# Batch 0's attention with fewer TensorE instructions and its local AV chunk by chunk; batch 1's v by two kinds of transfer

## The chip, the cores and the metric

The kernel runs on one core of a Trainium2 chip. The metric is the device time of one execution in microseconds; before the change the median of five runs is 331.19 us (329.89 to 333.34). Five engines take part: TensorE (PE; its weight loads are shown as PEld), VectorE (DVE), ScalarE (ACT), GpSimd (POOL) and SyncE (SP). Each works through its own list of instructions in order and waits for the others by semaphores. Transfers are issued by SyncE or by GpSimd and run on 16 DMA engines.

## The reference

Eight batches, eight heads, 576 tokens, head width 64. The attention is the sum of two softmax attentions: one over tokens averaged in groups of four (144 x 144), whose result is repeated four times, and one over the band of tokens less than four apart. Its output, 4608 tokens of 512, goes through two products with a gate between them.

```python
q_d = q.reshape(B, H, Sd, factor, D).mean(axis=3)        # likewise k_d, v_d; factor 4
out_up = np.repeat(sm_attn(q_d, k_d, v_d), factor, axis=2)
mask = np.abs(pos[:, None] - pos[None, :]) < factor
scores = np.where(mask, scale * q @ k.T, -1e9)
out_local = softmax(scores) @ v
x = (out_up + out_local)                                  # to (4608, 512)
h = x @ w_in                                              # (4608, 2048)
g = h * (1.0 / (1.0 + np.exp(-1.702 * h)))
out = g @ w_out                                           # (4608, 512)
```

## The kernel before

All matrix work is in bf16. The order of every engine's instructions is the order in which the program issues them (a manual schedule): nothing is moved by a scheduler.

**Tiling.** Of a batch, heads are taken in two groups of four ("qd", 0 and 1) for scores and in four pairs ("hp", 0 to 3) for the products with v. The local attention cuts the 576 tokens into ten blocks of about 57 queries with 64 keys: five chunks i, each with a half par 0 and a half par 1 that lie in the lower and upper 64 partitions. `scores` (L340) makes 80 small matmuls for a group, `scores_d` (L362) 24 for the averaged attention. `av_local` (L403) makes 20 matmuls for a pair, four per chunk, and `av_down` (L417) 20 for the averaged part. Both write one tile of PSUM; a column of ones in v gives the softmax's sum, and `normalise` (L439) divides on VectorE. The tiles of PSUM are PA[0..2], two banks each, and PM[0..1].

**Batch 0.** It has nothing to hide behind and is written out by hand (L712 to L800). k and q come by casting transfers from GpSimd, v by ten transfers from SyncE (`load_v`, L207: five chunks, two halves each). VectorE transposes k and q (`prep_1`, L256); GpSimd adds tokens in fours (`pool_qk`, L270). Constants come from iotas on GpSimd and comparisons on VectorE: the mask of the band, an identity `ident` of 64 columns, once in each half of the partitions, the selection matrix `psel` (`make_psel`, L164, and `end_psel`, L180) and the matrix `up` (`make_up` and `spread_up`). In batch 0 the band is made by TensorE: `bar_others` (L327) writes −1e6 outside the band into the tiles of scores by eight matmuls with `ident`, four for each half, and the scores add to it. v's chunks are cast to bf16 by ScalarE (0 and 1) and VectorE (2 to 4); `prep_vd_pe` (L306) makes the averaged v from all five chunks by 14 matmuls with `psel`, and ScalarE copies it to SBUF. Then come `av_local` and `av_down` of pairs 0 and 1, `scores_d` of the second group, pairs 2 and 3, and between them `turned` (L782): it transposes a pair's result, adds the repeated part by `transp_sum` (L477) and has it copied to `xT`, the input of the dense products. `warm(n)` (L570) issues n matmuls of 512 columns on zeros whose result is not used; it is called with 19, 5, 6 and 1.

**Dense products.** Group g of 512 tokens goes through `mm1` (w_in, L618; Silu on ScalarE, L629) and `mm2` (w_out, L674; copies on ScalarE, L659). The attention of batch g+1 is put between these matmuls at positions listed in POS (in POS_0 for g = 0, where `prep_vd_pe` of batch 1 stands at 52).

**Loads around group 0** (L808 to L823). GpSimd's list: w_in, k and q of batch 1, the first half of w_out, a memset of v4 (L740), then for g = 0 the adding in fours for batch 1, a one-element copy that waits for batch 1's v to land in part (the gate, L814, chunk 3), the second half of w_out, five casts of v 1's chunks, and the loads of k and q of batch 2. SyncE's list: v of batch 0, v of batch 1 (ten transfers behind a gate on the first part of w_out), then v of batch 2, which waits until the casts have read v 1.

Of the kernel before, what the change touches and what calls it, by code (L numbers as in the profile page):

```python
# [19 lines left out]
def kernel(  # L20
# [32 lines left out]
        tc.tile_pool(name="psum", bufs=1, space=bass.MemoryType.PSUM)  # L53
    )

    ident = consts.tile([128, 64], BF16, name="ident")
    mask = consts.tile([128, 2, 300], BF16, name="mask")
    w_in_bf = persist.tile([128, n_dmc, d_ff], BF16, name="w_in_bf")
    w_out_bf = persist.tile([128, n_ffc, d_model], BF16, name="w_out_bf")
# [28 lines left out]
    PSEL = [(4, 2), (2, 1), (0, 0), (1, 0), (1, 1), (3, 1), (3, 2)]  # L88

    dm = consts.tile([128, 60], FP32, name="dm")  # L90
    di = consts.tile([128, 64], FP32, name="di")
    dr = consts.tile([128, 1], FP32, name="dr")
    du = consts.tile([128, UP], FP32, name="du")
    ub = consts.tile([128, UP], BF16, name="ub")
# [13 lines left out]
    def iota_mask():  # L108
        for par in range(2):
            nc.gpsimd.iota(dm[halves[par]], pattern=[[-1, 60]], base=-4 * par,  # L110
                           channel_multiplier=1, **it)
        for par in range(2):
            nc.gpsimd.iota(di[halves[par]], pattern=[[-1, 64]], base=0,
                           channel_multiplier=1, **it)

    def iota_up():
        for par in range(2):
# [17 lines left out]
    def make_mask():  # L135
# [7 lines left out]
            in_=dm[:, None, :].to_broadcast([128, 10, 60]),  # L143
        )

    def make_ident(di):
        nc.vector.tensor_single_scalar(out=ident, in_=di, scalar=0.0, op=ALU.is_equal)

    def make_up():
        nc.vector.reduce_sum(out=rm, in_=ident[:, 0:48], axis=mybir.AxisListType.X)  # L150
        nc.vector.scalar_tensor_tensor(
            out=du, in0=du, scalar=-192.0, in1=du, op0=ALU.add, op1=ALU.mult
        )
        nc.vector.tensor_scalar(
            out=ub, in0=du, scalar1=0.0, scalar2=rm, op0=ALU.is_equal, op1=ALU.mult
        )
# [47 lines left out]
        load_1("k", k, kf, b, qd)  # L204
        load_1("q", q, qf, b, qd)

    def load_v(b, gate=None):  # L207
        t = ldp.tile([128, 5, H, D], FP32, name="vf", tag="vf")
        vf[b] = t
        if gate is not None:  # L210
            gate(t[0:1, 0, 0, 0:1])
        for i in range(5):
            for par in range(2):
                nc.sync.dma_start(
                    out=t[64 * par : 64 * par + 64, i],
                    in_=bass.AP(
                        tensor=v.tensor,
                        offset=v[b, 0].offset + (114 * i + KSTART[par]) * D,
                        ap=[[D, 64], [S * D, H], [1, D]],
                    ),  # L220
                )

    def load_v4(b):
        for kc in range(3):
# [100 lines left out]


    def bar_others(sp):  # L327
        for par in range(2):
            rows = slice(64 * par, 64 * par + 64)
            for r in range(4):  # L330
                nc.tensor.matmul(
                    sp[r // 2][rows, r % 2, 0:300],
                    lhsT=ident[rows, :],
                    rhs=off[rows, None, :].to_broadcast([64, 5, 60]),
                    start=True, stop=True,
                    tile_position=(64 * par, 64 * par),
                    skip_group_check=True,
                )

    def scores(b, qd, barred=False):  # L340
        sp = [ps_tile(), ps_tile()]
# [58 lines left out]
        av_down(b, hp, o)  # L400
        return o

    def av_local(b, hp, o):  # L403
        E, vb = es[hp], vbs[b % 2]
        for i in range(5):
            for par in range(2):
                for j in range(2):
                    pos = j if par == 0 else 1 - j
                    nc.tensor.matmul(  # L409
                        o[64 * pos : 64 * pos + 64, par, 65 * i : 65 * i + 65],  # L410
                        lhsT=E[64 * par : 64 * par + 64, j, 60 * i : 60 * i + 64],
                        rhs=vb[64 * par : 64 * par + 64, i, 2 * hp + j, :],
                        start=True, stop=True,
                        tile_position=(64 * par, 64 * pos),
                    )
# [34 lines left out]
    def transp(y, n=None):  # L450
        x = ps_tile(n)
        for i in range(5):
            for par in range(2):
                for j in range(2):
                    pos = j if par == 0 else 1 - j
                    c0 = 0 if (par == 1 or i == 0) else 3
                    c1 = 60 if (par == 0 or i == 4) else 57
                    nc.tensor.matmul(  # L458
                        x[64 * j : 64 * j + 64, par, 57 * i + c0 : 57 * i + c1],
                        lhsT=y[64 * pos : 64 * pos + 60, par, i, :],  # L460
                        rhs=ident[64 * pos : 64 * pos + 60, c0:c1],
                        start=True, stop=True,
                        tile_position=(64 * pos, 64 * j),
                    )
        for c2, xx in ((0, 0), (0, 1), (1, 0)):
            for j in range(2):
                pos = j if xx == 0 else 1 - j
                nc.tensor.matmul(
                    x[64 * j : 64 * j + 64, xx, 288 + 48 * c2 : 336 + 48 * c2],
                    lhsT=y[64 * pos : 64 * pos + 48, j, 5 + c2, :],  # L470
                    rhs=ident[64 * pos : 64 * pos + 48, 0:48],
                    start=True, stop=True,
                    tile_position=(64 * pos, 64 * j),
                )
        return x

    def transp_sum(y, x):  # L477
# [24 lines left out]
        for i in range(5):  # L502
            for par in range(2):
                for j in range(2):
# [3 lines left out]
                    nc.tensor.matmul(  # L508
                        x[par][64 * j : 64 * j + 64, 57 * i + c0 : 57 * i + c1],
                        lhsT=y[64 * pos : 64 * pos + 60, par, i, :],  # L510
                        rhs=ident[64 * pos : 64 * pos + 60, c0:c1],
                        start=False, stop=True,
                        tile_position=(64 * pos, 64 * j),
                        skip_group_check=True,
# [52 lines left out]

    def warm(n):  # L570
        if n:
            t = pm_tile()
            for _ in range(n):
                nc.tensor.matmul(  # L574
                    t, lhsT=wz[:, 0:128], rhs=wz, start=True, stop=True
                )

    def attention(b, slots=None):
# [139 lines left out]
    iota_up()  # L718
    fill()
    load_v(0, gate=after(kdT[1][0:1, SD, 0:1], nc.vector))  # L720
    warm(19)
    make_mask()
    make_ident(di)
    prep_1("k", 0, 0)
    prep_1("q", 0, 0)
    pool_qk(0, 0)
    sp = scores(0, 0, barred=True)
    exp_local(0, sp)
    prep_qk(0, 1)
    pool_qk(0, 1, "k")  # L730
    nc.gpsimd.tensor_copy(out=w_in_bf[0:1, 0, 0:1], in_=vf[0][0:1, 2, 0, 0:1])
    load_w_in(0, 512)
# [4 lines left out]
        load_qk(1, qd)  # L737
    load_w_out(0)
    load_w_out(1)
    nc.gpsimd.memset(v4[32:64], 0.0)  # L740
    make_psel()
    end_psel()
    make_up()
    warm(5)
    sd = scores_d(0, 0)
    prep_v(0, nc.scalar, i=slice(0, 1))
    exp_down(0, sd)
    sp = scores(0, 1, barred=True)
    exp_local(1, sp)
    prep_v(0, nc.scalar, i=slice(1, 2))  # L750
    spread_up()
    for i in range(2, 5):
        prep_v(0, nc.vector, i=slice(i, i + 1))
    warm(6)
    prep_vd_pe(0, PA[2])
    for hp in range(2):
        o[hp] = PA[hp]
        av_local(0, hp, o[hp])
    for hp in range(2):
        av_down(0, hp, o[hp])  # L760
        y[hp] = normalise(o[hp])
# [4 lines left out]
            func=AF.Exp, scale=inv_sqrt_d / 16.0,  # L766
        )
    nc.scalar.preload_act_table_set("silu_and_others")
    warm(1)
    o[2] = av(0, 2, 2)  # L770
    y[2] = normalise(o[2])

# [33 lines left out]
    for g in range(n_groups):  # L806
        b = g + 1
        if g == 0:  # L808
            prep_qk(1, 0)
            pool_qk(1, 0)  # L810
            prep_qk(1, 1)
            load_v(1, gate=after(w_out_bf[0:1, 0, 0:1], nc.vector))
            pool_qk(1, 1)
            nc.gpsimd.tensor_copy(  # L814
                out=w_out_bf[0:1, 8, 0:1], in_=vf[1][0:1, 3, 0, 0:1]
            )
            load_w_out(2)
            load_w_out(3)
            for i in range(5):
                prep_v(1, nc.gpsimd, i=slice(i, i + 1))  # L820
            for qd in range(NQ):
                load_qk(2, qd)
# [54 lines left out]
```

The softmax here doesn't subtract the row's maximum and nothing guards it: scores larger than these inputs give would overflow.

## Time and profile before

| | |
|---|---|
| median of five runs | 331.19 us |
| the profiled execution | 330.17 us |
| its span, first to last instruction | 328.4 us |
| TensorE busy | 96% of the span |
| granted TensorE clock, mean | 0.995 |
| ScalarE, VectorE, GpSimd busy | 56%, 40%, 42% |
| DMA, mean | 126 GB/s, 41.36 MB |

The profile shows one execution. A line such as `14.62 0.18 PE L351 MATMUL ... x1 [1.41 <-issue]` of the timeline reads: from 14.62 us on, 0.18 us long, TensorE executed line 351, once, after having been idle for 1.41 us; the arrow names what ended the idle time, and "issue" means that the engine waited for nothing which the profile shows. In a table of windows each row gives a stretch of time, its length, then the busy microseconds of each engine with the number of instructions, then the granted TensorE clock as a share of full speed, the busy share of the DMA engines and the GB/s. The chain in order of time gives start, length and what was at work in the chain that ended last.

The first 67 us hold the part in which TensorE has gaps: batch 0's attention until about 30.5 us, from where dense products run, and batch 1's attention between 42.7 and 67.3 us.

### The profile page before, as it was taken

To read this page: it belongs to the slowest core of one execution; us is meant where nothing else is said; L and a number is where in the kernel's file an instruction comes from. 1 tells how busy PE (TensorE), PEld (TensorE's weight loads), DVE (VectorE), ACT (ScalarE), POOL (GpSimd) and SP (SyncE) were. 2 spreads that over 40 slices of the span, in tenths; PEclk is the share of its full clock that TensorE was granted. 3 is DMA by queue.
4 is the path that set the end of the run, shared out by engine and by line. 5 is a ranking of instruction groups with operands and counts; after the bars stand their busy time and mean duration, and the time that the engine had idled before them with its cause. 6 is when DMAs were issued, how large, how long until landed. Compare 5 with 4: busy or idle time off the path is not lost.

```text
span 328.4 us, 11276 instructions
## 1 busy us (share of the span) xinstructions
PE 313.7 (96%) x5043; PEld 157.8 (48%) x5043; DVE 131.7 (40%) x215; ACT 184.1 (56%) x322; POOL 138.3 (42%) x168
## 2 busy tenths in 40 slices
PE   8777999899999999999999999999999999999995
PEld 3453455435554455445544554454444544444444
DVE  4872423670477037803680378125730560000000
ACT  2552882465926593658366836774576656415611
POOL 7890843069505960397039802990098000000000
PEclk9989999999999999999999999999999999999999
DMA  7999979999616980499139913992180100021011
GB/s 125 184 200 208 166 153 190 187 263 221 157 36 169 215 166 36 132 208 188 56 116 205 198 67 103 204 195 83 53 159 2 68 34 32 2 77 51 2 63 65
DMA packets 63552, 41.36 MB, mean 126 GB/s; under 512 B 44048, under 2 KB 54416, under 8 KB 63504
## 3 DMA queue, kind: packets, MB, share of 16 engines
q1 hardware_dynamic: 55056, 26.95, 34.5%
q0 software_dynamic: 8304, 13.63, 23.6%
q8 instruction: 39, 0.64, 0.8%
q14 instruction: 9, 0.07, 0.1%
q10 hardware_dynamic: 144, 0.07, 0.1%
HBM read 44.83 MB, written 9.44 MB: 165 GB/s over the span
## 4 chain that ended last, share of the span: by engine, by line
PE 91%; issue 3%; DMA 2%; DVE 2%; ACT 1%; POOL 1%; POOLq 0%; ACTq 0%; DVEq 0%
PE pm L618 36%; PE pm L674 36%; PE pa L351 4%; DMA qb<-in_q_dram 2%; PE pa L618 2%; PE pa L431 2%; PE pa L409 2%; PE pa L458 2%; PE pa L370 2%; PE pa L674 2%; PE pm L689 1%; PE pm L574 1%; PE pa L312 1%; ACT vd L321 0%; DVE xT L555 0%
## 5 line engine op out<-in xcount | busy, mean ns | idle before, releaser
L618 PE MATMUL pm<-xT,w_in_bf 128*128 128x512 bf16 x544 | 121.3, 379 | 0.7 <-DVE xT L561 0.7
L674 PE MATMUL pm<-w_out_bf,gT 128*128 128x512 bf16 x528 | 121.7, 380 | 0.0
L629 ACT ACTIVATE gT<-pm 128x512 bf16<-128x512 f32 x136 | 81.0, 598 | 45.3 <-PE pm L618 45.3
L618 PEld LDWEIGHTS <-w_in_bf 128*128 128x128 bf16 x576 | 55.6, 98 | 67.7 <-issue 1.4
L674 PEld LDWEIGHTS <-gT 128*128 128x128 bf16 x560 | 51.7, 98 | 59.5 <-issue 0.2
L276 POOL TENSOR_TENSOR pq<-kT 128x576 f32<-128x576 bf16 x16 | 18.5, 1157 | 103.6 <-DVE kT L260 95.4
L395 DVE TENSOR_TENSOR es<-es,mask 128x600 bf16<-128x600 bf16 x28 | 21.5, 785 | 92.3 <-ACT es L381 91.6
L659 ACT ACTIVATE osb<-pm 128x512 f32<-128x512 f32 (+2 forms) x35 | 20.7, 593 | 40.1 <-PE pm L674 36.1
L534 ACT COPY od<-pa 128x384 f32<-128x384 f32 (+1 forms) x56 | 18.4, 412 | 32.0 <-DVE y L444 18.7
L444 DVE TENSOR_TENSOR y<-pa,rc 128x896 bf16<-128x896 f32 x32 | 34.9, 1092 | 1.1
L555 DVE TENSOR_TENSOR xT<-pa,od 128x570 bf16<-128x570 f32 x28 | 21.1, 754 | 11.6 <-ACT od L534 11.5
L381 ACT ACTIVATE es<-pa 128x600 bf16<-128x600 f32 x32 | 19.8, 668 | 7.4 <-PE pa L351 7.2
L297 POOL TENSOR_TENSOR v<-v 112x512 f32<-112x512 f32 x18 | 22.8, 1266 | 0.0
L661 DVE TENSOR_SCALAR osb<-pm 128x128 f32<-128x128 f32 x1 | 0.3, 291 | 55.3 <-ACT osb L659 55.3
L260 DVE STREAM_TRANSPOSE kT<-kb 128x576 f32<-128x576 f32 x16 | 20.0, 1249 | 1.7 <-DMA kb<-in_k_dram 1.7
L260 DVE STREAM_TRANSPOSE qT<-qb 128x576 f32<-128x576 f32 x16 | 19.8, 1240 | 1.1 <-DMA qb<-in_q_dram 1.1
L276 POOL TENSOR_TENSOR pq<-qT 128x576 f32<-128x576 bf16 x16 | 18.4, 1148 | 0.0
L291 POOL CAST vb<-vf 128x2560 bf16<-128x2560 f32 (+1 forms) x11 | 17.2, 1592 | 0.0
L351 PE MATMUL pa<-qT,kT 32*64 32x60 bf16 x1280 | 14.4, 203 | 2.3 <-issue 1.4
L351 PEld LDWEIGHTS <-kT 32*64 32x64 bf16 x1280 | 12.3, 104 | 7.6 <-issue 6.3
L442 DVE RECIPROCAL rc<-pa 128x14 f32<-128x14 f32 x32 | 7.7, 240 | 20.5 <-PE pa L431 20.5
L300 POOL TENSOR_TENSOR vd<-v 112x256 bf16<-112x256 f32 x18 | 13.7, 759 | 1.4
(90 smaller groups left out, 246.5 us busy)
## 6 DMA issues: line engine op xcount, KB each, us to landing
vf<-in_v_dram SPq DMA_DIRECT2D x80, 128.0 KB, 5.3
out_dram<-osb SPq DMA_DIRECT2D x35, 256.0 KB, 2.0
v<-in_v_dram SPq DMA_DIRECT2D x36, 192.0 KB, 5.1
kb<-in_k_dram POOLq DMA_DIRECT2D x16, 288.0 KB, 6.3
qb<-in_q_dram POOLq DMA_DIRECT2D x16, 288.0 KB, 7.9
w_out_bf<-in_moe_w_out_dram POOLq DMA_DIRECT2D x4, 512.0 KB, 12.5
w_in_bf<-in_moe_w_in_dram POOLq DMA_DIRECT2D x2, 512.0 KB, 6.5
w_in_bf<-in_moe_w_in_dram POOLq DMA_DIRECT2D x1, 1024.0 KB, 10.6
```

Source lines behind the costliest of these rows:

```text
L260: nc.vector.transpose(out=t32.rearrange("p (i c) -> p c i", c=18), in_=store[b, qd].bitcast(FP32).rearrange("p (c d) -> p c d", c=18),)
L276: nc.gpsimd.tensor_tensor(out=t1, in0=sv[:, :, 0:2, :], in1=sv[:, :, 2:4, :], op=ALU.add)
L297: eng.tensor_tensor(out=t1[0:112], in0=x[:, :, 0:2, :], in1=x[:, :, 2:4, :], op=ALU.add)
L351: nc.tensor.matmul(sp[r // 2][64 * par : 64 * par + 64, r % 2, 60 * i : 60 * i + 60], lhsT=kT[b, qd][rows, k0 : k0 + 64, a], rhs=qT[b, qd] ...
L381: nc.scalar.activation(out=es[2 * qd + u][:, :, 0:300], in_=sp[u][:, :, 0:300], func=AF.Exp, scale=inv_sqrt_d,)
L395: nc.vector.tensor_tensor(out=ev, in0=ev, in1=mask, op=ALU.mult)
L444: nc.vector.tensor_tensor(out=y, in0=ov[:, :, :, 0:D], in1=rc.to_broadcast([128, 2, 7, D]), op=ALU.mult,)
L555: eng.tensor_tensor(out=sub(xT[hp], t0 + 3, (57, 2), (114, 5), (1, 57)), in0=sub(x, 3, (509, 2), (57, 5), (1, 57)), in1=sub(od, 3, (57, 2) ...
L618: nc.tensor.matmul(acc, lhsT=w_in_bf[:, dmc, ffc * 128 : (ffc + 1) * 128], rhs=xT[dmc][:, g * TG : g * TG + TG], start=(dmc == 0), stop=(d ...
L629: nc.scalar.activation(out=gT[:, ffc, :], in_=acc, func=AF.Silu, scale=GELU_SCALE)
L659: eng.activation(out=osb, in_=ap, func=AF.Copy, scale=1.0 / GELU_SCALE)
L674: nc.tensor.matmul(ops[t], lhsT=gT[:, ffc, t * 128 : (t + 1) * 128], rhs=w_out_bf[:, ffc, :], start=(ffc == 0), stop=(ffc == n_ffc - 1),)
```

## The change

The identity becomes one of 128 columns over all 128 partitions (`id128`), and `ident(pos, n, c0, c1)` gives the 64-wide parts that the transposes read. `bar_others` then makes four matmuls over all partitions in place of eight over halves. `warm` is called with 11, 4 and 3 in place of 19, 5 and 6, the call with 1 is gone, and the first of the 11 reads `id128` as its weights; it stands behind `make_ident`. VectorE runs `make_psel` between the transposes of k and q of the second group. The cast of v 0's chunk 1 moves from ScalarE to VectorE. `av_local` of pairs 0 and 1 is issued for chunks 0 to 3 ahead of `prep_vd_pe`, and for chunk 4 after it. Of v 1, SyncE loads chunks 0 to 2 and GpSimd casts them; chunks 3 and 4 come by four casting transfers that GpSimd issues (`load_vb`), straight into the bf16 tile. The gate of w_out's second half reads chunk 1 of v 1 in place of chunk 3. The memset of v4 moves in the source into the g = 0 branch; on GpSimd it stays between w_out's first half and the adding in fours.

```diff
-    ident = consts.tile([128, 64], BF16, name="ident")
+    id128 = consts.tile([128, 128], BF16, name="id128")
...
+    def ident(pos, n, c0, c1):
+        return id128[64 * pos : 64 * pos + n, 64 * pos + c0 : 64 * pos + c1]
...
+    def load_vb(b, i):
+        for par in range(2):
+            nc.gpsimd.dma_start(
+                out=vbs[b % 2][64 * par : 64 * par + 64, i, :, 0:D],
+                in_=bass.AP(
+                    tensor=v.tensor,
+                    offset=v[b, 0].offset + (114 * i + KSTART[par]) * D,
+                    ap=[[D, 64], [S * D, H], [1, D]],
+                ),
+            )
...
-        for par in range(2):
-            rows = slice(64 * par, 64 * par + 64)
-            for r in range(4):
-                nc.tensor.matmul(
-                    sp[r // 2][rows, r % 2, 0:300],
-                    lhsT=ident[rows, :],
-                    rhs=off[rows, None, :].to_broadcast([64, 5, 60]),
-                    start=True, stop=True,
-                    tile_position=(64 * par, 64 * par),
-                    skip_group_check=True,
-                )
+        for r in range(4):
+            nc.tensor.matmul(
+                sp[r // 2][:, r % 2, 0:300],
+                lhsT=id128,
+                rhs=off[:, None, :].to_broadcast([128, 5, 60]),
+                start=True, stop=True,
+                skip_group_check=True,
+            )
...
-    def av_local(b, hp, o):
+    def av_local(b, hp, o, chunks=range(5)):
...
-    def warm(n):
+    def warm(n, first=False):
         if n:
             t = pm_tile()
-            for _ in range(n):
+            for m in range(n):
                 nc.tensor.matmul(
-                    t, lhsT=wz[:, 0:128], rhs=wz, start=True, stop=True
+                    t, lhsT=id128 if first and m == 0 else wz[:, 0:128], rhs=wz,
+                    start=True, stop=True,
                 )
...
-    warm(19)
     make_mask()
     make_ident(di)
+    warm(11, first=True)
...
-    prep_qk(0, 1)
+    prep_1("k", 0, 1)
+    make_psel()
+    prep_1("q", 0, 1)
...
-    nc.gpsimd.memset(v4[32:64], 0.0)
-    make_psel()
     end_psel()
     make_up()
-    warm(5)
+    warm(4)
...
-    prep_v(0, nc.scalar, i=slice(1, 2))
     spread_up()
-    for i in range(2, 5):
+    for i in range(1, 5):
         prep_v(0, nc.vector, i=slice(i, i + 1))
-    warm(6)
+    warm(3)
+    for hp in range(2):
+        o[hp] = PA[hp]
+        av_local(0, hp, o[hp], range(4))
     prep_vd_pe(0, PA[2])
     for hp in range(2):
-        o[hp] = PA[hp]
-        av_local(0, hp, o[hp])
+        av_local(0, hp, o[hp], range(4, 5))
...
-    warm(1)
...
         if g == 0:
+            nc.gpsimd.memset(v4[32:64], 0.0)
+            load_vb(1, 3)
+            load_vb(1, 4)
             prep_qk(1, 0)
...
-            load_v(1, gate=after(w_out_bf[0:1, 0, 0:1], nc.vector))
+            load_v(1, gate=after(w_out_bf[0:1, 0, 0:1], nc.vector), chunks=range(3))
...
-                out=w_out_bf[0:1, 8, 0:1], in_=vf[1][0:1, 3, 0, 0:1]
+                out=w_out_bf[0:1, 8, 0:1], in_=vf[1][0:1, 1, 0, 0:1]
...
-            for i in range(5):
+            for i in range(3):
                 prep_v(1, nc.gpsimd, i=slice(i, i + 1))
```

## Prediction

> **What bounds the kernel now.** I read the page's first three parts, then the chain that ended last, then TensorE's timeline up to 67 us, then tables of windows. The page first: TensorE is busy 96% of the span, and it executes 10,088 instructions (5,043 weight loads, 5,043 matmuls, two others), which come in through a queue of their own.
>
> ```profile
> PE 313.7 (96%) x5043; PEld 157.8 (48%) x5043; DVE 131.7 (40%) x215; ACT 184.1 (56%) x322; POOL 138.3 (42%) x168
> q8 instruction: 39, 0.64, 0.8%
> ```
>
> 0.64 MB over 10,088 instructions is 63 bytes each, and over 39 packets 16 KB, so a packet is a page of 256 instructions. From 67 us on TensorE hardly pauses, and the change leaves that part's work as it is. What can be won lies before. The chain in order of time names two gaps there in which TensorE waits for nothing that the profile shows, and a third at 63 us:
>
> ```profile
> 13.21 1.41 issue
> 24.02 2.72 issue
> 63.31 0.89 issue
> ```
>
> TensorE's timeline shows what stops: the middle of a series without any dependence between its members.
>
> ```profile
> 14.62 0.18 PE L351 MATMUL pa<-qT,kT 32*64 32x60 bf16 x1 [1.41 <-issue]
> 23.77 0.25 PE L508 MATMUL pa<-ident,y 60*64 60x60 bf16 x6
> 26.74 0.31 PE L508 MATMUL pa<-ident,y 60*64 60x57 bf16 x14 [2.72 <-issue]
> ```
>
> Counted in the program, those two places are instructions 448 and 960, and the third is 2240: 448 + 2·256 and 448 + 7·256. They are page ends. The packets of the instruction queue fit: in the trace they start at 11.80, 18.51, 24.51 and 30.45 us, take 0.94 to 1.33 us, and TensorE resumes 1.5 and 1.3 us after the first and the third end. The three pages follow one another at about 6 us. [...] All this is while the DMA engines are full (share 1.0 to 1.2).
>
> [...]
>
> **Front part, step by step.** The change removes 42 instructions ahead of the dense products: 8+1+3+1 warming matmuls (26 instructions), 4 matmuls in each of two bar_others (16). Page ends stay at 448 and 960 of the count, and so fall on work that stood 42 later.
>
> *Stall of 1.41 us.* Instruction 448 is now in hp 0's fourth v chunk, work that has to wait for v's casts anyway. The stall in the scores goes. What is late next: DVE's order. make_psel (12.18 to 13.76, 1.58 us) moves ahead of the q 1 transpose, which could start at 11.07: k 1's is over at 10.05, so q 1's starts at 11.63, 0.56 us late, and scores(0, 1) end at 13.8 in place of 14.8. The casts of v on DVE no longer wait for the 1.97 us of L151, which sat beside POOL's 14.07 to 16.05; but v's last transfer lands at 16.91, so the last cast ends at 17.4 against 18.2. prep_vd_pe, ACT's copy (0.80) and av_down come 0.8 us earlier. ACT loses one cast of 0.61, DVE gains one of 0.42: both inside this wait. The wider iota, identity and reduce cost 0.1 each at most, beside loads.
>
> *Stall of 2.72 us.* It stood at 960; there now stands the work that ran at 27.73 (within turned(2), L484 from 27.52), so at the same arrival of the page 27.73 − 26.74 = 1.0 us is won. Against it: the first request. warm(11) now reads id128, ready at 4.5 us (L147 starts at 4.19, 0.29 us), where before TensorE started at 1.20. Behind that wait stand the bars and scores(0, 0), and behind those exp on ACT. Its clock rose at 4.85, 3.65 us after the start. From 4.6 at 0.43 us a matmul (half clock, as the nine before 4.85 show) to about 8.3, then 0.22, eleven end at 8.8; four full-width bars of 300 columns, 0.13 each, end at 9.3; scores(0, 0) begin 0.85 us after the 8.49 of before, the request goes out at 9.9, 1.0 us later. With three pages of 6 us behind it, 960 is there at 27.7, and the 1.0 us is spent. The range is wide: the clock can rise between about 6.5 and 9.7, which puts the sum between −0.7 and +0.8. I take 0. The earlier vd then only lengthens the waits at 704 (to 21.7) and 960 (24.2 to 27.7, 3.4 us).
>
> **The clock.** The windows before the dense part:
>
> ```profile
> core 0: us, PE busy (x) PEld busy (x) DVE busy (x) ACT busy (x) POOL busy (x), PEclk, DMA share, GB/s
> 11.68:15.09 3.41, 1.74 (x90) 1.17 (x86) 3.31 (x10) 2.22 (x4) 2.18 (x5) 1.00 0.97 165
> 15.09:18.50 3.41, 3.41 (x20) 1.60 (x17) 3.08 (x5) 1.94 (x3) 3.33 (x5) 0.50 1.02 158
> 25.33:28.74 3.41, 2.00 (x50) 1.21 (x50) 0.00 (x0) 1.13 (x6) 0.00 (x0) 1.00 1.12 209
> 28.74:32.16 3.42, 3.42 (x45) 1.77 (x44) 1.04 (x3) 0.99 (x6) 0.00 (x0) 1.00 1.11 210
> ```
>
> 1.74 us busy of 3.41 is followed by half clock, 2.00 by full. [...] In this execution the stall fell 1.31/1.41 across a border and the clock held; shifted, it loses a window at half clock, up to 1.7 us in dense work. That would explain why the profiled execution (330.17 = span 328.4 + 1.8 around it) lies 1.0 under the median of 331.19. After the change the stall of some 3.4 us brings the loss in nearly every execution, about 1.3 us. So from the profiled time +1.3, from the median +0.3. The fewer warming matmuls after 15 us cost at half clock only in stretches that wait for a page: nothing on the path.
>
> **Middle, 36 to 67 us.** For v 1, SyncE issues 6 transfers in place of 10 and POOL casts 3 chunks in place of 5 (0.62 each, −1.2 us on POOL). POOL issues four more (between 0.55 of kb and 0.84 of w_in each: 2.2 to 3.4 us), which wait in order for older transfers, the last landing at 31.09; POOL stands idle until 32.96 (8.12 us for DVE's kT), so this is covered; uncovered it would push pool_qk(1, 0) by up to 3.4 us, of which scores at 42.7 leave most free. The casting transfers queue behind w_out's, landed at 39.39; half a MB at about 200 GB/s makes 43, needed at 53.2. If casting in small pieces goes at half that rate, 45. The gate of w_out's second half opens on v 1's chunk 1 (42 to 43) instead of 3 (45.17), and the loads for batch 2 follow about 3 us earlier; no TensorE row waits for them, gain 0. The 2.65 us memset stays at its place in POOL's order.
>
> The page ends move by 42 here too. 1984 falls in the second tr instead of the first. Its request slips out of the dense products (50.1) into prep_vd_pe (53.5): 21 pairs at 0.216 us. With 6 us it is there at 59.7, wanted at 58.4: a stall of 1.3 us that did not exist, and 2240 asks after it, 0 to 0.8 us of stall in place of 0.89. Net +0.4 to +1.2; with less DMA traffic −0.9. I take +0.6.
>
> **Late.** Two gaps of the same kind, at 123.53 (0.37) and 224.46 (0.78), lie in av, at 4288 and 7872. 42 on, the page ends meet dense products 1 us later: −1.15; between −1.15 and 0 if other ends grow. I take −1.15.
>
> Sum from the median: 331.19 + 0 + 0.3 + 0.6 − 1.15 = 330.9; from the profiled time: 330.17 + 0 + 1.3 + 0.6 − 1.15 = 330.9.
>
> **Rivals.**
> *Faster, requests not late.* If the clock rises at 6.5 to 7, scores(0, 0) keep their 8.49, the page comes at 26.8 and 1.0 us is won; if the earlier transfers also shorten the pages near 60 us, another 0.8. 330.9 − 1.8 = 329.1. For it: the page latency at quiet DMA, in the later batches, is about 1.1 us to the packet against 3 to 4 here. Against: the engines stay full until 35 us.
> *Slower, the page of 1984.* One mechanism: its request moves 3.4 us later, because a dense stretch that covered it ends before it. It decides from a latency of 4.9 us (58.4 − 53.5); the page of 2240 took 6.9 in the same stretch. At 6.9 it costs 2.0, hands the full lateness to 2240, and nothing shrinks: +2.1 against the +0.6 taken, with the clock then falling once more (+0.8): 333.2.
> *It doesn't do what it says.* Half the removed instructions are warming ones beside waits; if the pages weren't the cause, nothing moves: 331.2, inside the first case.
>
> **Numbers.** About as before (330.9): 0.55; faster rival 0.22; slower rival 0.20 (333.2); v 1's casting transfers or something unseen late by 4 us or more (335): 0.03. 80% lies between 328.8 and 333.4. A measurement of this kernel can tell about 1% from no change, 3.3 us: faster by more (under 327.9) 0.08, the far end of the faster rival; slower by more (over 334.5) 0.07, the end of the slower one and the last case; within 0.85.
>
> **What would show it.** Right: no gap in scores(0, 1); scores(0, 0) at 9.0 to 9.8; a gap of over 3 us in turned(2), ending between 27 and 28.3, then a window at half clock; a gap in the second tr at 58 to 60; none at 123 and 224. Wrong: a gap at 960 under 2 us, or warm(11) ending by 7.5. What would upset the number: another page latency in the first 30 us, since three of them stand in a row.

## The result and the profile after

The change makes no difference that can be told: 331.3 us (median; 329.3 to 335.5) against 331.4 us for the kernel before, measured beside it, a ratio of 1.0004 with a 95% interval of 0.9991 to 1.0018. The ratios here and below leave out executions that took over 1.5% longer than the fastest of their kernel; the medians do not. The profiled execution took 330.80 us, span 329.0, against 330.17 and 328.4. The forecast was 330.9. That this is not the same as "nothing happened" shows already in the page. First TensorE's and the instruction queue's lines, then the granted clock in 40 slices of 8.2 us:

```profile
PE 313.5 (95%) x5022; PEld 158.5 (48%) x5022; DVE 132.2 (40%) x216; ACT 183.6 (56%) x321; POOL 140.7 (43%) x169
PEclk9857999999999999999999999999999999999999
q8 instruction: 39, 0.64, 0.9%
```

42 instructions are gone, and the clock is at 0.8, 0.5 and 0.7 in slices 2 to 4, where the kernel before had one short dip; its mean over the span is 0.979 in place of 0.995. The stalls have moved as well. The chain of after in order of time, those of its "issue" steps in which TensorE stood still (start, length):

```profile
28.48 0.59 issue
...
59.83 0.59 issue
...
90.58 0.22 issue
...
191.48 1.00 issue
```

Both long stalls of the front, 1.41 and 2.72 us, and those at 63, 123 and 224 us are gone. One of 0.59 is left at instruction 960, one of 0.59 is new in the second `tr`, one of 1.00 is new at 191, and a short one of 0.22 at 91. TensorE's timeline of after says what stands in the place of the first two; the bracket gives idle time and releaser:

```profile
4.44 0.61 PE L586 MATMUL pm<-wz,id 128*128 128x512 bf16 x1 [4.44 <-DVE id L148]
...
9.12 0.84 PE L363 MATMUL pa<-qT,kT 32*64 32x60 bf16 x80
...
13.67 0.83 PE L363 MATMUL pa<-qT,kT 32*64 32x60 bf16 x80 [1.63 <-DVE qT L275]
16.82 0.27 PE L421 MATMUL pa<-vb,es 64*64 64x65 bf16 x4 [0.96 <-DVE vb L306]
17.62 0.83 PE L421 MATMUL pa<-vb,es 64*64 64x65 bf16 x24 [0.53 <-DVE vb L306]
20.98 0.87 PE L443 MATMUL pa<-vd,ed 48*64 48x65 bf16 x40 [0.64 <-ACT vd L336]
29.07 0.16 PE L506 MATMUL pa<-up,y 128*64 128x3 bf16 x1 [0.59 <-issue]
```

These are waits for VectorE, for v's casts and for ScalarE's copy of vd. Together with a clock that stays at half speed they bring TensorE late to instruction 960, so that the page, there at about 29 us, is hardly waited for. The table of windows (columns as before: length, busy time of the engines, clock, DMA) shows how long half clock holds:

```profile
11.30:14.72 3.42, 1.79 (x95) 1.30 (x87) 3.38 (x8) 1.41 (x3) 2.24 (x4) 1.00 1.35 179
14.72:18.13 3.41, 1.84 (x28) 0.66 (x30) 3.41 (x5) 2.23 (x3) 3.31 (x4) 0.50 1.01 147
18.13:21.54 3.41, 2.77 (x79) 2.06 (x76) 0.31 (x1) 0.80 (x1) 3.41 (x7) 0.50 1.13 167
21.54:24.96 3.42, 3.22 (x111) 2.57 (x107) 3.23 (x6) 2.19 (x3) 3.38 (x3) 0.50 1.16 211
24.96:28.37 3.41, 3.41 (x95) 2.19 (x86) 1.93 (x3) 1.70 (x9) 0.99 (x2) 0.50 1.12 211
28.37:31.78 3.41, 2.82 (x70) 1.67 (x64) 0.00 (x0) 0.83 (x4) 1.36 (x2) 1.00 1.12 211
```

Four windows at half clock, 14.71 to 28.37 us, against one, 15.09 to 18.50, before. In both kernels half clock follows a window busy for about half its length (1.74 before, 1.79 after). Before, the next window was busy throughout (3.41 of 3.41: warming matmuls and `prep_vd_pe`) and full clock came back at once. After, the next three are busy 54%, 81% and 94%, none of them brings it back, and the fourth, busy 100%, does.

Where the two profiled executions stand against one another (start of the same matmul in both, us):

| | before | after | later by |
|---|---|---|---|
| scores(0, 0) | 8.49 | 9.12 | 0.63 |
| last matmul of scores(0, 1) | 14.62 | 14.29 | −0.33 |
| last small matmul ahead of the dense products | 30.38 | 31.72 | 1.34 |
| first scores of batch 1 | 42.69 | 44.03 | 1.34 |
| prep_vd_pe of batch 1 | 53.21 | 54.42 | 1.21 |
| last matmul | 324.6 | 325.5 | 0.9 |

So the front loses 1.34 us in this pair, the middle and the late part win 0.4, and 0.3 more is won behind the last matmul.

### The profile page after: what moved, and what is told of

It is laid out like the page before. It is cut to its first block, busy times and chain, and to the rows that moved or that the text cites. A ratio compares the mean times of both kernels' runs of the same rounds, so it can differ in the third digit from the quotient of the medians.

```text
span 329.0 us, 11227 instructions
## 1 busy us (share of the span) xinstructions
PE 313.5 (95%) x5022; PEld 158.5 (48%) x5022; DVE 132.2 (40%) x216; ACT 183.6 (56%) x321; POOL 140.7 (43%) x169
## 4 chain that ended last, share of the span: by engine, by line
PE 90%; DMA 2%; SPq 2%; issue 2%; DVE 2%; ACT 1%; DVEq 0%; ACTq 0%
PE pm L631 36%; PE pm L687 35%; PE pa L363 3%; PE pa L421 2%; PE pa L631 2%; PE pa L443 2%; DMA vf<-in_v_dram 2%; SPq L218 2%; PE pa L470 2%; PE pa L382 2%; PE pa L687 2%; PE pm L702 1%; PE pa L327 1%; PE pa L496 1%; PE pa L480 0%
## 5 line engine op out<-in xcount | busy, mean ns | idle before, releaser
L407 DVE TENSOR_TENSOR es<-es,mask 128x600 bf16<-128x600 bf16 x28 | 20.6, 751 | 91.4 <-ACT es L393 90.6
L306 POOL CAST vb<-vf 128x2560 bf16<-128x2560 f32 (+1 forms) x9 | 16.1, 1806 | 0.0
L421 PE MATMUL pa<-vb,es 64*64 64x65 bf16 x640 | 12.8, 202 | 2.8 <-DVE vb L306 1.5
```

Of the source, the lines that this page charges most:

```text
L407: nc.vector.tensor_tensor(out=ev, in0=ev, in1=mask, op=ALU.mult)
```

## The experiments

The theory at the outset was that of the prediction: pages of instructions set the stalls, the clock follows them, and v 1's transfers weigh nothing. The rivals: that the clock, through the waits for VectorE and the casts, sets the front; and that one of the edits loses by its place what another wins. All kernels do the whole computation. The mean clock of an execution tells how long it ran at half: one window of 3.41 us takes 0.0052 off it (the profiled executions: 0.995 with one such window before, 0.979 with four after). The last column is worked out so, as a mean over all executions of that kernel; the kernel before, measured again beside each group, has 1.6 to 2.1.

| kernel | median us | ratio to before, 95% interval | half-clock windows |
|---|---|---|---|
| after | 331.3 | 1.0004 (0.9991 to 1.0018) | 4.4 |
| e1_psel_later | 331.6 | 1.0022 (0.9998 to 1.0046) | 4.1 |
| e2_warm_fill | 333.0 | 1.0045 (1.0021 to 1.0069) | 3.4 |
| e3_v1_only | 330.3 | 0.9982 (0.9955 to 1.0009) | 2.1 |
| e4_pad42 | 332.6 | 1.0032 (1.0007 to 1.0057) | 5.1 |
| e5_warm12 | 332.5 | 1.0056 (1.0037 to 1.0074) | 2.1 |
| e6_old_warm | 333.3 | 1.0068 (1.0044 to 1.0093) | 3.8 |
| e8_front_only | 332.7 | 1.0064 (1.0040 to 1.0089) | 4.6 |
| e9_warm6 | 331.3 | 1.0009 (0.9986 to 1.0031) | 2.8 |
| e10_v1_only_again | 330.3 | 0.9969 (0.9944 to 0.9994) | 1.5 |
| e11_bars_v1 | 332.4 | 1.0054 (1.0034 to 1.0075) | 4.0 |
| e12_chunks_v1 | 330.5 | 0.9991 (0.9960 to 1.0022) | 3.1 |

**e1_psel_later**: after, with make_psel behind q 1's transpose again.

```diff
-    prep_1("k", 0, 1)
-    make_psel()
-    prep_1("q", 0, 1)
+    prep_qk(0, 1)
...
+    make_psel()
     end_psel()
```

> The kernel after, with make_psel back behind the transpose of q 1, where it stood before the change. In the profile of after, make_psel took 9.76 to 12.45 us and q 1's transpose, whose data had landed at 10.5, started at 12.37. Theory 1 (pages: the dense products start when the page of instruction 960 is there): q 1's transpose starts at 10.5 to 11, scores(0, 1) 1.3 us earlier than 13.67, the gap at 960 grows by as much as is won, and the last small series before the dense products (turned(3)) ends at 31.8 within 0.4; time as after within 0.3. Theory 2 (the clock and VectorE set the start): scores(0, 1) close the idle window, the clock holds after 15 us, and turned(3) ends 1.0 to 1.5 us earlier; time 1.0 to 1.5 us less.

The last matmul of scores(0, 1) started at 13.55 in place of 14.29, and then TensorE waited 2.53 us for v's casts, which VectorE began at 16.82, straight from the operation before. Neither theory's time for the front came out: the last small matmul ahead of the dense products started at 34.02 in place of 31.72, after five windows at half clock. The two kernels differ by 0.18%, less than the runs can tell.

**e2_warm_fill**: after, with six warming matmuls between the bars and scores(0, 1), where TensorE waits for q's transpose.

```diff
         if barred:
             bar_others(sp)
+            warm(6 if qd else 0)
```

> The kernel after, with six warming matmuls more (12 instructions) between the second bars and scores(0, 1), where TensorE sat idle for 1.63 us. Theory 1 (pages): the granted clock stays at full speed between 15 and 28 us, the small series in front of 960 get done up to 1.5 us earlier, and the gap at 960 grows from 0.59 to 2 us or more; turned(3) ends at 31.8 within 0.4 and the time is that of after within 0.4. Theory 2 (clock): turned(3) ends at 30.5 or earlier, time 1.0 to 1.5 us less than after.

Half clock began later (19.50 in place of 14.71) but again lasted 13.65 us, and the last small matmul of the front started at 33.74, 2.0 us later than in after and later than both theories had it. Filling that wait moves the fall of the clock to the next one, and costs time.

**e3_v1_only** and **e10_v1_only_again**: the kernel before with the v 1 part alone.

```diff
+            load_vb(1, 3)
+            load_vb(1, 4)
             prep_qk(1, 0)
...
+            load_v(1, gate=after(w_out_bf[0:1, 0, 0:1], nc.vector), chunks=range(3))
...
+                out=w_out_bf[0:1, 8, 0:1], in_=vf[1][0:1, 1, 0, 0:1]
...
+            for i in range(3):
```

> The kernel before with one part of the change alone: v 1 by six SyncE transfers and four casting transfers of GpSimd, the gate on chunk 1. No TensorE instruction is taken away. Expected by the prediction's sum: no gain and no loss (0 within 0.3 us); w_out's second half issued 1 to 3 us earlier than 45.72, no TensorE row waits for v 1, and the gap of page 2240 stays near the 0.89 of before. Rival (the middle won through earlier transfers): that gap is under 0.3 and the time 0.6 us or more below before.

> The kernel before with the v 1 part alone, as in the run of that name, once more. If the gain of the first run (0.9982) is real: 0.997 to 0.9995, about 330.3 to 331 us, by the stall at 2240 gone. If it was chance: 0.9995 to 1.002.

0.9982 and 0.9969, the second clear of 1: a gain of about 0.25%, 0.8 us. In both traces the front keeps its stalls (1.43 and 2.77; 1.61 and 2.69 us), and the stall of 0.89 at instruction 2240 has shrunk; the chain of e3_v1_only has there

```profile
64.19 0.27 issue
```

and that of e10_v1_only_again has nothing. A stall of 0.54 at 90 us is new in both.

**e8_front_only**: after without the v 1 part (all of v 1 by SyncE, five casts, the gate on chunk 3).

> The changed kernel with the v 1 part undone: all ten transfers of v 1 by SyncE, five casts on GpSimd, the gate on chunk 3; batch 0 as changed. If the two parts add up (v 1 part about -0.2%, front about +0.2 to +0.3%): 331.9 to 332.5 us, 1.001 to 1.004 of the kernel before; half clock over about four windows, with the end of the small series near 31.7 us as in the changed kernel. If the v 1 part is worth nothing: the same time as the changed kernel, 331.3 to 331.6. If the front part alone is a gain and the v 1 part spoils it: under 330.5.

1.0064: batch 0's edits alone are a loss, and the v 1 part is worth 0.6% beside them, against 0.25% alone. So the parts do not simply add up. TensorE's timeline shows one place of it, in the second `tr` of batch 1; first e8_front_only, then after:

```profile
61.51 0.21 PE L470 MATMUL pa<-id,y 60*64 60x60 bf16 x1 [1.34 <-issue]
```

```profile
60.42 0.21 PE L470 MATMUL pa<-id,y 60*64 60x60 bf16 x1 [0.59 <-issue]
```

At the same instruction the stall is 1.34 without the casting transfers and 0.59 with them: the packet of that page started 2.84 us after TensorE had entered the page before it, in place of 2.11. What makes it quicker is not shown; the DMA engines are as full in both from 56 to 60 us (share 1.12 in e8_front_only, 1.12 to 1.15 in after).

**e4_pad42**: after, with 21 pairs of one-column instructions in front, so that the page ends fall on the work on which they fell before the change.

```diff
             t = pm_tile()
+            for m in range(21 if first else 0):
+                nc.tensor.matmul(
+                    t[0:32, 0:1], lhsT=wz[:, 0:32], rhs=wz[:, 0:1], start=True, stop=True
+                )
```

> The kernel after with 21 matmuls of one column and their weight loads (42 instructions) put in front of the first warming matmul, where TensorE waits for the identity until 4.4 us. They cost no time themselves, but every page end falls on the work on which it fell before the change. Theory 1 (pages): gaps at the old places: at the end of scores(0, 1), in turned(1) (2 us or more in place of 0.59), in av at 123 and 224 us or near; turned(3) ends 0.5 to 1.2 us later than 31.84, and the time is 0.5 to 1.5 us above after. Theory 2 (clock): no change beyond 0.3 us.

1.0032, and half clock for five windows (15.29 to 32.36). The late stalls went back to the instructions at which the kernel before has them, and those at 91 and 191 shrank to 0.20 and 0.22. TensorE's timeline of e4_pad42:

```profile
125.97 0.28 PE L443 MATMUL pa<-vd,ed 48*64 48x65 bf16 x7 [0.53 <-issue]
...
192.98 0.31 PE L443 MATMUL pa<-vd,ed 48*64 48x65 bf16 x14 [0.22 <-issue]
...
227.45 0.35 PE L443 MATMUL pa<-vd,ed 48*64 48x65 bf16 x17 [0.33 <-issue]
```

So the late stalls follow the instruction count. In the front they did not. There was no stall in scores(0, 1), and 0.70 at 960 in place of 2.72, since TensorE was late there anyway. The time rose by about what the first theory had written, but not by the stalls that it named.

**e5_warm12** and **e9_warm6**: after, with 12 or 6 in place of 3 warming matmuls behind scores(0, 1).

```diff
-    warm(3)
+    warm(12)
```

> The kernel after, with 12 warming matmuls in place of 3 behind scores(0, 1), where TensorE then waits for the casts of v until 16.8 us (18 instructions more). Theory 1 (pages): the clock keeps full speed from 15 us on and the small series reach instruction 960 before 26 us, but its page comes at 28 to 29.5 as in after; the gap there is 2.5 us or more, one window at half clock follows it, and the dense products' preparation (end of turned(3)) is over at 31 to 32, as in after's 31.72. Theory 3 (what the runs before this one suggest: the time at half clock sets the end, and it ends only with a window that is busy throughout): less than 7 us at half clock, the end of turned(3) 1.5 us or more ahead of the 33.3 to 34.0 of the kernels with 17 us at half clock; time 0.5 to 1.5 us under that of e1_psel_later measured before (331.6).

> The changed kernel with 6 warming matmuls in place of 3 behind scores(0, 1), as the kernel before has. My theory is that half clock ends only after a fully busy window: three more matmuls fill the window from 18.1 (0.81 busy in the changed kernel), so full clock comes back at about 21.5 in place of 28.4. Then TensorE is early again and waits for the page of 960 (2 to 3 us, until 28 to 29), which drops the clock once more after it. The time: 331.3 to 332.5. Half-clock windows 3 to 4 in place of 4.3. If the clock alone made the loss, under 330.5; if the extra matmuls lie on the path at half clock (3 x 0.43 us), 332.5 to 333.

With 12 the clock was full from 9.69 to 26.75 us, and TensorE's timeline of e5_warm12 shows what that bought:

```profile
14.84 2.54 PE L586 MATMUL pm<-wz 128*128 128x512 bf16 x11 [0.16 <-issue]
...
28.00 0.26 PE L520 MATMUL pa<-id,y 60*64 60x60 bf16 x2 [3.66 <-issue]
```

A stall of 3.66 us at 960: TensorE was there at 24.3 and the page at 28. It is the stall that the prediction had at this place (3.4). With half clock the time goes into slow matmuls, with full clock into the page, at which work goes on between 26 and 30 us in all these traces. e9_warm6 has 1.6 windows fewer than after on average and the same time; the profiled execution of it still ran four windows at half clock (18.55 to 32.20). The added matmuls ran ahead of the first of them, which was busy 81% as in after, so the early return that I expected of six did not come there.

**e6_old_warm**: e1 with the warming calls of before (19, 5, 6, 1, the first without id128).

```diff
-    warm(11, first=True)
+    warm(19)    # ahead of make_mask()
...
-    warm(4)
+    warm(5)
...
-    warm(3)
+    warm(6)
...
+    warm(1)
```

> The kernel after with all of the warming matmuls of before (19, 5, 6 and 1, the first not waiting for the identity) and make_psel behind the transpose of q 1; the wider bars, the local AV chunk by chunk and v 1's two kinds of transfer stay (16 instructions fewer than before in place of 42). Against e1_psel_later only the warming differs. Theory 3 (clock): at most one or two windows at half clock, the end of turned(3) at 30.4 to 31.5, time 0.8 to 1.5 us under e1_psel_later, equal to or up to 1 us under before. Theory 1 (pages alone): the page of 960 stands 26 instructions earlier in the work than in e1_psel_later; time equal to it or up to 0.6 us above.

1.0068, against 1.0022 for e1: taking the warming matmuls out is the part of the front that wins, about 0.46%. The theory that the clock sets the time had expected one or two windows at half clock and a gain of 0.8 to 1.5 us here; there are 3.8 windows, and a loss. TensorE waited 1.79 us for the casts and 1.67 us at 960.

**e7_late_loads**: after, with the second half of w_in, k and q of batch 1 and the first half of w_out issued behind `y[1]`, at about 24 us, to see the page without that traffic.

> A measurement, not a version: the kernel after with the second half of w_in, k and q of batch 1 and the first half of w_out issued by GpSimd only behind batch 0's second normalise (some 24 us) in place of 18.2 to 22.6. The DMA engines are less full between 18 and 24 us. Theory 1 (a page is late because the engines are full): the packets of pages 704 and 960 start 1.0 to 2.5 us after the request in place of 5.0 and 3.9, page 960 is there by 26.5 in place of 29.0 and there is no gap at it. Rival (the latency is the queue's own): they start 3.5 us or more after the request as before. The time says nothing: the weights come late.

No record shows when a page is asked for, so I count from TensorE's first instruction of the page before. The packet of the page of 960 started 0.4 us after it (23.47 to 23.87; in after 23.36 to 26.66, 3.3 us), and there was no stall at 960. For the page of 704, with the DMA engines still full (share 1.12 from 18.13 to 21.54), it was 1.2 us against 1.8 in after. By this count after's two are 1.8 and 3.3 us, not the 5.0 and 3.9 of the expectation. A window of the stretch, whose last two numbers are the DMA share and GB/s, to be held against 1.16 and 211 in after:

```profile
21.54:24.96 3.42, 3.22 (x111) 2.58 (x107) 3.11 (x6) 2.08 (x3) 0.20 (x2) 0.50 0.37 62
```

So in this pair of traces the page is late where the traffic is. The loads are then missing later (5.33 us of stall at 45 us in the chain; single time 334.8).

**e11_bars_v1** and **e12_chunks_v1**: the kernel before with the v 1 part and one part of the front: e11 the identity of 128 columns and four bars (the matmuls of `bar_others`) in place of eight; e12 the local AV chunk by chunk with the cast of chunk 1 on VectorE.

```diff
# e11
-        for par in range(2):
-            rows = slice(64 * par, 64 * par + 64)
-            for r in range(4):
...
-                    lhsT=ident[rows, :],
...
+        for r in range(4):
...
+                lhsT=id128,
# e12
+        av_local(0, hp, o[hp], range(4))
     prep_vd_pe(0, PA[2])
     for hp in range(2):
-        o[hp] = PA[hp]
-        av_local(0, hp, o[hp])
+        av_local(0, hp, o[hp], range(4, 5))
```

> The kernel before with the v 1 part and, of the front, only the identity of 128 columns with four bars over all partitions in place of eight (16 instructions fewer ahead of the dense products); warming matmuls, psel, the cast of chunk 1 and the order of the local AV as before. It is the earlier run with the old warming calls, less the local AV chunk by chunk, and that run took 1.0068. If the local AV chunk by chunk is what loses: 0.996 to 1.000 here, as the v 1 part alone (0.9969), with half clock for one or two windows and turned(3) over at 31 to 32 us. If the bars lose (their page ends fall worse): 1.003 to 1.008 here.

> The kernel before with the v 1 part and, of the front, only the local AV of pairs 0 and 1 chunk by chunk ahead of prep_vd_pe, with the cast of chunk 1 on VectorE; eight bars, warming matmuls and psel as before, so no instruction is removed and the page ends stay at the same counts. If the chunk order is what loses: 1.003 to 1.008, with TensorE waiting about 1.8 us for the casts at 17 us, a window only half busy there, so half clock from 18 to 20 us on for two windows or more, and turned(3) over at 33 us or later. If it is harmless or a gain: 0.994 to 1.000.

The chunk order shows no loss (0.9991, interval to 1.0022). The four bars, 16 instructions fewer, lose: 1.0054 against 0.9969 and 0.9982 without them. TensorE's timelines, first e10_v1_only_again, then e11_bars_v1:

```profile
14.88 0.18 PE L362 MATMUL pa<-qT,kT 32*64 32x60 bf16 x1 [1.61 <-issue]
...
17.59 0.30 PE L323 MATMUL pa<-vb,psel 128*64 128x256 bf16 x2 [0.65 <-DVE vb L302]
18.12 0.63 PE L323 MATMUL pa<-vb,psel 128*64 128x256 bf16 x6 [0.22 <-DVE vb L302]
...
26.73 0.40 PE L519 MATMUL pa<-ident,y 60*64 60x57 bf16 x14 [2.69 <-issue]
```

```profile
16.91 0.30 PE L327 MATMUL pa<-vb,psel 128*64 128x256 bf16 x2 [1.52 <-DVE vb L306]
17.72 0.85 PE L327 MATMUL pa<-vb,psel 128*64 128x256 bf16 x6 [0.50 <-DVE vb L306]
...
27.97 0.31 PE L520 MATMUL pa<-id,y 60*64 60x57 bf16 x6 [1.73 <-issue]
```

The stall of 1.61 us in the scores is gone, as meant: their last matmul starts at 12.92 in place of 14.88. Of those 2 us hardly anything is left behind the next wait. The casts come only 0.4 us earlier, so TensorE waits 2.02 us for them in place of 0.87, at 17 us in both. What holds the first of VectorE's casts is not v's landing (both halves of its chunk 2 are there at 14.96 and 15.14) but VectorE's own list. Its timelines, first e10_v1_only_again, then e11_bars_v1, have no idle time ahead of the casts:

```profile
14.46 2.08 DVE L151 SCALAR_TENSOR_TENSOR du<-du 128x245 f32<-128x245 f32 x1
16.57 0.63 DVE L154 TENSOR_SCALAR ub<-du,rm 128x245 bf16<-128x245 f32 x1
17.12 1.27 DVE L302 CAST vb<-vf 128x512 bf16<-128x512 f32 x3
```

```profile
14.84 1.68 DVE L158 TENSOR_SCALAR ub<-du,rm 128x245 bf16<-128x245 f32 x1
16.44 1.56 DVE L306 CAST vb<-vf 128x512 bf16<-128x512 f32 x3
```

One of the two operations of `make_up` takes 2.08 or 1.68 us there, the other 0.63 or 0.41. And the window that holds the wait is emptier. Windows of e10_v1_only_again, then of e11_bars_v1:

```profile
13.15:16.57 3.42, 1.65 (x25) 0.69 (x15) 3.35 (x7) 1.89 (x4) 2.38 (x4) 1.00 0.82 133
16.57:19.98 3.41, 2.08 (x91) 1.38 (x89) 1.82 (x4) 1.81 (x2) 3.41 (x6) 1.00 1.15 175
```

```profile
14.12:17.54 3.42, 1.45 (x10) 0.53 (x9) 3.38 (x6) 1.78 (x3) 3.06 (x4) 1.00 0.85 138
17.54:20.95 3.41, 3.04 (x110) 2.53 (x109) 1.27 (x4) 0.82 (x2) 3.41 (x6) 0.50 1.20 182
```

Busy 48%, and the clock held; busy 42%, and it fell, for four windows, to 31.19. The last small matmul started 1.07 us later (32.87 against 31.80). e12 has its fall too (40% busy, then 10.24 us at half clock), but reaches 960 at 27.7, just as the page comes, and stands there for 0.2 us at most. Its last small matmul starts at 31.82, as in e10_v1_only_again, with three windows at half clock in place of one.

**What the parts are worth.** The kernels make a chain from before to after, one part at a time, each step the quotient of two ratios above:

| step | change |
|---|---|
| before → v 1 part (mean of e3, e10) | −0.25% |
| → identity of 128 columns, four wide bars (e11) | +0.79% |
| → local AV chunk by chunk, cast moved (e6) | +0.14% |
| → fewer warming matmuls (e1) | −0.46% |
| → make_psel earlier (after) | −0.18% |
| sum | +0.04% |

Each step is uncertain by about 0.3% (two intervals put together). The bars' loss and the warming matmuls' gain are clear of that, the v 1 part by its two runs, the other two are not. The steps hold in this order only: taken last, the v 1 part is worth 0.6% (e8_front_only). The kernel before with the v 1 part alone is the fastest here, 330.3 us.

## Why the prediction was right, and where it was not

The number was right to 0.4 us, by a sum whose terms were partly wrong. From the profiled time it had +0 for the stalls of the front, +1.3 for the clock, +0.6 for the middle, −1.15 late: +0.75. The profiled execution shows +1.34 at the end of the front, −0.2 from there to 68 us, −0.2 more until the last matmul: +0.9, and +0.63 in the time.

**The clock step failed in its mechanism.** The prediction said that one window is lost behind a stall of 3.4 us in turned(2), and that "the fewer warming matmuls after 15 us cost at half clock only in stretches that wait for a page: nothing on the path". Measured: four windows at half clock, beginning already at 14.71, behind the wait of 1.63 us for q's transpose; the waits for the casts (0.96 and 0.53) fall into the first of them. The step took half clock to end with any window of work. Here it ended, in every trace shown, only behind windows busy for nine tenths or more (91% in e11_bars_v1 the least). That the front's loss came out at 1.34 where 1.3 was written is chance: against the median, where the step had +0.3, the executions have 4.4 windows in place of 1.6 to 2.1. Sorted by windows, after took 330.0, 331.2, 332.3 and 334.4 us with three, four, five and six, and the kernel before 330.4 to 330.8 us with one and 330.9 to 332.0 with three, by the group of runs. So with as many windows after would be the faster kernel, by 1 to 2 us; it has some 2.5 more, and a window goes with 0.2 to 0.7 us in the kernel before and about 1.1 in after. That the windows cause the time, rather than both follow from the same waits, is argued and not shown: e5_warm12 and e9_warm6 have fewer windows than after and no less time, and e12_chunks_v1 has 1.3 more than the kernel before at the same time.

**The front stall** was given as 3.4 us and came out at 0.59, which by the prediction's own signs ("a gap at 960 under 2 us") is wrong. The page at 960 was late (27.7 written, 29.07 measured), but not by the way that was written. Its delay was to come from the first request. The packet of that first page, however, started at 11.94 against 11.80 before, and only the next two were late, 19.76 against 18.51 and 26.66 against 24.51: TensorE entered the page at 448, behind its waits for the casts, at 17.97 in place of 14.73. And TensorE came to 960 at 28.5, not at 24.2. e5_warm12, which keeps it in time, shows 3.66. No run shows when a page is asked for: the requests at 9.9, 50.1 and 53.5 us, from which the 27.7 and the stalls of 3.4 and 1.3 us are worked out, are the author's estimates. The traces show when the packets start, and that is not at one distance from TensorE's first instruction of the page before: in the trace of before 2.8, 3.8 and 2.9 us behind it for the pages of 448, 704 and 960, 0.4 us behind it for the page of 1984 (2.1 in after), and 2.0 us ahead of it for the page of 1472, in the dense products.

**scores(0, 0)** at 9.12 (predicted 9.0 to 9.8), the delay by `id128`, and no gap inside scores(0, 1) are right. **make_psel** was mis-sized. VectorE's timeline before, then after, and GpSimd's of after beside it:

```profile
11.07 1.26 DVE L260 STREAM_TRANSPOSE qT<-qb 128x576 f32<-128x576 f32 x1 [0.87 <-DMA qb<-in_q_dram]
...
12.83 0.16 DVE L171 SCALAR_TENSOR_TENSOR r<-dr,r 128x1 f32<-128x1 f32 x1
13.03 0.16 DVE L175 TENSOR_TENSOR rv<-rv,r 128x2 f32<-128x2 f32 x1
```

```profile
10.18 0.63 DVE L175 SCALAR_TENSOR_TENSOR r<-dr,r 128x1 f32<-128x1 f32 x1
10.84 1.07 DVE L179 TENSOR_TENSOR rv<-rv,r 128x2 f32<-128x2 f32 x1
11.84 0.61 DVE L180 SCALAR_TENSOR_TENSOR dp<-dp 128x448 f32<-128x448 f32 x1
12.37 1.25 DVE L275 STREAM_TRANSPOSE qT<-qb 128x576 f32<-128x576 f32 x1
```

```profile
10.13 0.67 POOL L300 TENSOR_TENSOR qdT<-pq 128x288 bf16<-128x288 f32 x1
10.75 1.15 POOL L291 TENSOR_TENSOR pq<-kT 128x576 f32<-128x576 bf16 x1
```

Two operations on one or two elements took 0.63 and 1.07 us in place of 0.16 each, each ending with a GpSimd operation (VectorE's at 10.81 and 11.91 us, GpSimd's at 10.80 and 11.90); before, GpSimd was idle beside them, from 12.71 to 13.54. What makes them end together is not shown. The q 1 transpose thus started at 12.37, not at 11.63. The next link failed the same way: "v's last transfer lands at 16.91, so the last cast ends at 17.4 against 18.2". It was VectorE's list that held the casts: the 1.96 us met L158 in place of L151 (beside GpSimd again, 14.47 to 16.43), the casts ended at 18.44, and nothing was won for vd.

**The middle** (+0.6) failed in its term for v 1, "gain 0". e10_v1_only_again and e8_front_only show a gain of 0.3 and 0.6%, of which the shorter stalls near 60 us, 0.6 to 0.9 us, are the part that the traces show. The gate of w_out's second half opened at 44.39 in place of 45.22, not by 42 to 43. The new stall at 1984 is where it was predicted, at 0.59 in place of 1.3, and 2240's is gone. **Late**, the stalls at 123 and 224 vanished as predicted, but others of the same kind came: 1.00 at 191 and 0.22 at 91, in place of the 1.15 won. e4_pad42 moves them back, so it is the count that places them; how long each lasts could not be read from the trace of before.

Of the rivals, the faster one failed at its condition: the page at 960 came later than 26.8, not at it. The slower one had the right place and the wrong size (0.59 where it had 2.0). "It doesn't do what it says" would have given the same time and is refuted by the traces: the instructions are gone, the stalls moved, and its parts by themselves move the time by up to 0.8%.

**Open.** The bars lose 0.8%, 2.6 us, of which the profiled pair shows only 1.07 us at the end of the front; the profiled execution of e11_bars_v1 was among its fastest (330.6). The rest is not in a trace. Whether the bars lose by where the page ends fall, which they move by 16 instructions, or by the emptier window and the clock was not tried apart; e4_pad42, in which the ends fall on the old work, is no faster than after.

## What to carry to other kernels

When a stall is taken away ahead of a wait that another engine's list sets, it turns up in that wait; follow the freed time to the next wait, and ask what sets it, before counting it. A wait that leaves about half of a clock window empty can be followed by half clock (1.79 of 3.41 us busy in after, then 13.65 us at half clock), until a window is nearly full (91% busy in e11_bars_v1, 100% in after). Instructions that fill it can cost time as well (e5_warm12: 2.1 windows at half clock in place of 4.4, and 332.5 us in place of 331.3), so neither warming matmuls nor their removal can be priced apart from what TensorE does behind them. Measure the parts of a change one by one when the whole shows no difference: here one of five parts lost about what two others won, and the last two were too small to tell.

## What the runs showed of the hardware

- **Return to full clock.** Windows at half clock that were busy 54%, 81% and 94% were followed by half clock again, one busy 100% by full clock (after). In other traces, in which about one in a hundred matmul records is missing, 89% was not enough and 91% was (e11_bars_v1), and 94% and 93% were not while another 94% was (e9_warm6). The half-clock windows of 91% to 94% that ended it (e5_warm12, e9_warm6, e10_v1_only_again, e11_bars_v1) held three to five matmuls of 512 columns, those of 89% to 94% that did not (after, e9_warm6, e11_bars_v1) none to two; whether busy time or these matmuls make the difference, no run here tells.
- **Fall to half clock.** It followed windows busy 21% (e10_v1_only_again), 40% (e12_chunks_v1), 42% (e11_bars_v1), 51% (before) and 52% (after), while others busy 48% (e10_v1_only_again), 59% and 62% (before) kept full clock, so the busy share alone does not decide in between.
- **A page of instructions under load.** From TensorE's first instruction of the page before to the packet of the page of 960 it took 3.3 us with the DMA engines full (share 1.16, after) and 0.4 us with their share at 0.37 (e7_late_loads).
- **Small VectorE operations beside GpSimd.** 0.16 us each with GpSimd idle (before, 12.83 and 13.03 us), 0.63 and 1.07 us beside it (after, 10.18 and 10.84), each ending with the GpSimd operation.
